# Three entries of a hand-written planner changed: ranks of the centring, the engine of one square, the load prices of one batch

## The chip, the cores and the metric

The kernel runs on one core of a Trainium2 chip. The core has TensorE (PE in the profile; PEld is its weight load), VectorE (DVE), ScalarE (ACT), GpSimd (POOL) and SyncE (SP, which here only issues DMAs). The metric is the device time of one execution in microseconds, as the median of five runs. One further execution is profiled.

## What is computed

Linear attention per batch and head, an RMS norm over each head, and on its result a feed-forward layer with the SoLU activation and a layer norm:

```
kv  = einsum('bhsd,bhse->bhde', k, v)            # 8 batches, 8 heads, 576 rows, 64 wide
out = einsum('bhsd,bhde->bhse', q, kv)
x   = out / sqrt(mean(out*out) + 1e-6) * g_norm  # per head; then 4608 tokens x 512
h   = x @ w_in                                   # 512 -> 1024
u   = h * softmax(h)
ln  = (u - mean(u)) / sqrt(var(u) + 1e-6) * g_ln
y   = ln @ w_out                                 # 1024 -> 512
```

## The kernel before

**Tiles and chunks.** The tokens go in nine chunks of 512: chunks 0 to 7 hold 512 rows of one batch each, and chunk 8 holds the last 64 rows of all batches. For a chunk `c`, `kv_mm` (L286) multiplies k and v into PSUM, `kv_copy` (L304, L306) casts the result to bf16, three copies for each half, `qT_mm` (L314) and `qT` (L321, L323) transpose q (chunks 4 to 8 use a transposing DMA from SP instead, L328), and `o_mm` (L348) multiplies. Then come a square on ScalarE (`sq`, L363), the mean by a matmul (`s_mm`, L369), `ln` and `ex` on ScalarE (L373, L377; chunk 0 uses one reciprocal root, L383) and `x` on VectorE (L390).

**The feed-forward part.** Each chunk has eight blocks `f` of 128 features. `h_mm(c, f)` (L471) is four matmuls, `exp(c, f)` (L479) runs on ScalarE, `u(c, f)` (L486) multiplies h by its exponential on VectorE, `usq(c, f)` (L495 on ScalarE, L497 on GpSimd) squares u, and `es(c, n)` (L503) adds two exponentials on GpSimd. When all of u, usq and es of a chunk are there, `sums(c)` (L537) adds them over the features by matmuls, `turn` and `stats` (L545 to L558, VectorE) and `rstd` (L562, L564, ScalarE) make one factor for each token. `out(c, m, half)` (L585) multiplies u by `w_out_sb` in two halves of four matmuls, `ob(c, m)` (L617) scales the result, and `store` (L626) sends it off from SP.

**Centring.** The mean over the features is taken out of the weights once: `w_mean` (L570) makes the mean of g_ln times w_out in a PSUM bank of the tag `out`, and eight `w_center(f)` (L576, VectorE) write `w_out_sb[:, f]`. `out(c, m, 0)` needs `w_center` 0 to 3, `out(c, m, 1)` needs 4 to 7, and the bank of the mean comes free with the last of them.

**Buffers.** PSUM has two banks for `h`, two for `out`, two for `o`, one for `s` and one for `misc`. `kv_mm(c)` for c > 1 takes `misc` and `s`. In SBUF there are three slots each for k, v and q, four for e, two each for u, usq, es and x.

**The order.** The order of the program on every engine is made by a small planner, `Plan.order` (L33 to L81). Each piece of work is added with its engine, a length, a rank, what it needs, and the buffers that it takes first or uses. The planner keeps a time at which each engine is free. It takes again and again the piece that could start first, and among those with the same start the one with the lower rank, and it writes that piece's instructions. These times are the planner's own; on the chip only the order remains, and each instruction waits for its real inputs.

**Loads in the planner.** A load on GpSimd's queue has a length (the issue) and a `load` (the transfer). All loads form one queue: a load ends at `queue = max(queue, t + length + 1.0) + load` (L72) and counts as landed some time later (L73). At most eight loads are under way (L55). Loads of k, v and q for batches 0 and 1 come in two halves, for the others whole. Two more things steer them: `behind` (L249) holds the loads of batch b until `h_mm(b - 3, ...)`, and from batch 5 on also until `gate(b - 1)` (L335), a tiny GpSimd copy that reads the last element of q of the batch before, so that GpSimd passes it only when that load has landed.

**Ranks and engines.** The rank of a piece is the chunk in which it is due, with the block in eighths: `h_mm(c, f)` has c + f/8, `u(c, f)` that plus 0.04, so `u(0, 6)` has 0.79 and `u(0, 7)` 0.915. The squares of chunk 0 have -0.6. `qT(1, hf)` (ACT) has -0.9 + 0.8 (0.12 + 0.1 hf), and `kv_mm(3)` 1.4.

The two expressions around which the change turns:

```
first=[] if g else [(name, b)], load=2.9 / n if b < 4 else 3.5)
...
engine = "act" if f in {0: (2, 4, 6, 7), 1: (), NC - 1: (1, 3, 5, 6, 7)}.get(c, (2, 6)) else "pool"
```

Of the kernel before, what the change touches and what calls it, by code (L numbers as in the profile page):

```python
# [18 lines left out]
class Plan:  # L19
# [13 lines left out]
    def order(self):  # L33
        free, done, queue, lanes, mode = {}, {}, 2.5, [], {}
        held = {tag: [] for tag in self.bufs}
        waiting = {n: set(p[4]) for n, p in self.pieces.items()}
        behind = {}
        for n, needs in waiting.items():
            for m in needs:
                behind.setdefault(m, []).append(n)  # L40
        ready = [n for n, needs in waiting.items() if not needs]
        order = []
        while ready:
            best = None
            for n in ready:
                engine, length, rank, fn, needs, first, load = self.pieces[n]
                t = max([free.get(engine, 0.0)] + [done[m] for m in needs])
                more = {}
                for key in first:
                    old = held[key[0]] + more.setdefault(key[0], [])  # L50
                    more[key[0]].append(key)
                    if len(old) >= self.bufs[key[0]]:
                        last = self.users[old[-self.bufs[key[0]]]]
                        t = max([t] + [done.get(m, 1e9) for m in last])
                if load and len(lanes) >= 8:  # L55
                    t = max(t, lanes[-8])
                if t < 1e8 and (best is None or (t, rank) < best[:2]):
                    best = (t, rank, n)
            t, rank, n = best
            engine, length, rank, fn, needs, first, load = self.pieces[n]  # L60
            ready.remove(n)
            for key in first:
                held[key[0]].append(key)
            if engine == "pe":

                tiling = n[0] if n[0] in ("kv_mm", "o_mm", "sums") else "full"
                length += 0.1 if mode.get(engine, tiling) != tiling else 0.0
                mode[engine] = tiling
            free[engine] = t + length
            done[n] = t + length + {"pe": 0.2, "sp": 2.5}.get(engine, 0.12) + (2.0 if n[0] == "qT" and engine == "sp" else 1.0 if n[0] == "gate" else 0.0)  # L70
            if load:
                queue = max(queue, t + length + 1.0) + load  # L72
                done[n] = queue + 1.3  # L73
                lanes.append(done[n])
            order.append(fn)
            for m in behind.get(n, ()):
                waiting[m].discard(n)
                if not waiting[m]:
                    ready.append(m)
        assert len(order) == len(self.pieces)  # L80
        return order  # L81
# [3 lines left out]
def kernel(  # L85
# [27 lines left out]
    NC = B + 1  # L113
# [19 lines left out]
    plan = Plan({**banks, **bufs})  # L133
# [105 lines left out]
    def heads(c):  # L239

        return (slice(0, 4), slice(4, 8)) if c < 2 else (slice(0, 8),)
# [5 lines left out]
    for b in range(B):  # L247
        at = b - 9.0 if b > 1 else (-2.0, -1.5)[b]
        behind = [] if b < 2 else [("h_mm", 0, 0)] if b == 2 else ([("gate", b - 1)] if b - 1 in XBAR else []) + [("h_mm", b - 3, 2 if b == 3 else 0)]  # L249
        for g, hs in enumerate(heads(b)):  # L250
            part = 0.1 * g
            n = len(heads(b))
            for i, (name, src) in enumerate((("k", k), ("v", v))):
                plan.add((name, b, g), "pool", 0.75 if n == 1 else 0.6, at + part + 0.01 * i,
                         lambda name=name, src=src, b=b, hs=hs: load_kv(name, src, b, hs),
                         behind, uses=[(name, b)] if g else [],
                         first=[] if g else [(name, b)], load=2.9 / n if b < 4 else 3.5)
            plan.add(("q", b, g), "pool", 0.9 if n == 1 else 0.7, at + part + (0.02 if b < 2 else 0.1),
                     lambda b=b, hs=hs: load_q(b, hs), behind,
                     uses=[("q", b)] if g else [], first=[] if g else [("q", b)], load=2.7 / n if b < 4 else 3.3)  # L260
        plan.add(("q_last", b), "pool", 0.6, 2.0 + 0.5 * b, lambda b=b: load_q_last(b),
                 [("h_mm", 2 + b // 2, 4 * (b % 2))], load=0.5)
    for half in range(2):
# [133 lines left out]
    for c in range(NC):  # L397
# [4 lines left out]
        if c < B:  # L402
            for xs in ((0,), (1,)) if c < 2 else ((0, 1),):
                g = xs[0]
                rg = r + 0.5 * w * g
                plan.add(("kv_mm", c, g), "pe", 0.65, rg, lambda c=c, xs=xs: kv_mm(c, xs), [("k", c, g), ("v", c, g)],
                         uses=[("k", c), ("v", c)], first=[(kv_tag(c, x), "kv", c, x) for x in xs])
                for x in xs:
                    for part in range(3):
                        plan.add(("kv", c, x, part), kv_engine(c, x), 0.25, rg + 0.05,  # L410
                                 lambda c=c, x=x, part=part: kv_copy(c, x, part), [("kv_mm", c, g)],
                                 uses=[(kv_tag(c, x), "kv", c, x)])
        if c in XBAR:
            plan.add(("qT", c), "sp", 1.8, r - 0.1, lambda c=c: q_turn(c),
                     [("q", c, 0)] if c < B else [("q_last", b) for b in range(B)],
                     uses=[("q", c)] if c < B else [], first=[("qT", c)])
# [3 lines left out]
        for hf in range(2):  # L420
            g = group(c, hf)
            tag = ("out", "h")[c] if c < 2 and hf else "o"
            if c not in XBAR:
# [7 lines left out]
                         first=[] if hf else [("qT", c)])  # L431
# [3 lines left out]
                     uses=[("qT", c)], first=[(tag, c, hf, z) for z in range(2)])  # L435
            for z in range(2):
                i = (c, hf, z)
                rz = r + w * (0.4 + 0.5 * hf + 0.12 * z)
                if (c, hf) in COPIED and z:
                    plan.add(("oc", i), "dve", 0.62, rz, lambda i=i: o_copy(*i), [("o_mm", c, hf)],  # L440
                             uses=[(tag, *i)], first=[("oc", i)])
                    plan.add(("sq", i), "pool", 1.05, rz + 0.01, lambda i=i: o_sq_copy(*i), [("oc", i)],
                             uses=[("oc", i)], first=[("osq", i)])
                else:
                    plan.add(("sq", i), "act", 0.57, rz, lambda i=i: o_sq(*i), [("o_mm", c, hf)],
                             uses=[(tag, *i)], first=[("osq", i)])
                stag = "h" if i in ((0, 0, 1), (0, 1, 0)) else "s"
                plan.add(("s_mm", i), "pe", 0.22, rz + 0.02, lambda i=i, stag=stag: s_mm(i, stag), [("sq", i)],
                         uses=[("osq", i)], first=[(stag, i)])
                if c == 0:  # L450
                    plan.add(("ex", i), "act", 0.6, rz + 0.04, lambda i=i: s_rsqrt(*i), [("s_mm", i)],
                             uses=[(stag, i)], first=[("rst", i)])
                else:
                    plan.add(("ln", i), "act", 0.6, rz + 0.03, lambda i=i: s_ln(*i), [("s_mm", i), "table"],
                             uses=[(stag, i)], first=[("lss", i)])
                    plan.add(("ex", i), "act", 0.6, rz + 0.04, lambda i=i: s_exp(*i), [("ln", i)],
                             uses=[("lss", i)], first=[("rst", i)])
                plan.add(("x", i), "dve", 0.67, rz + 0.06, lambda i=i: x_mul(*i),
                         [("ex", i)] + ([("x", (c, 0, 0))] if (hf, z) != (0, 0) else []),
                         uses=[(tag, *i), ("rst", i)] + ([("x", c)] if (hf, z) != (0, 0) else []),  # L460
                         first=[("x", c)] if (hf, z) == (0, 0) else [])
# [44 lines left out]
    for c in range(NC):  # L506
        for f in range(NF):
            r = c + f / 8
            plan.add(("h_mm", c, f), "pe", 0.87, r, lambda c=c, f=f: h_mm(c, f),
                     [("w_in", f // 4), *[("x", (c, *i)) for i in xs]], uses=[("x", c)], first=[(h_bank(c, f), "h", c, f)])  # L510
            plan.add(("exp", c, f), "act", 0.57, r + 0.02, lambda c=c, f=f: h_exp(c, f),
                     [("h_mm", c, f), "table"] + ([("exp", c, f - 1)] if f % 2 else []), uses=[(h_bank(c, f), "h", c, f)] + ([("e", c, f // 2)] if f % 2 else []),
                     first=[] if f % 2 else [("e", c, f // 2)])
            plan.add(("u", c, f), "dve", 0.62, r + 0.04, lambda c=c, f=f: h_u(c, f),
                     [("exp", c, f)] + ([("u", c, 0)] if f else []), uses=[(h_bank(c, f), "h", c, f), ("e", c, f // 2)] + ([("u", c)] if f else []),
                     first=[] if f else [("u", c)])
            engine = "act" if f in {0: (2, 4, 6, 7), 1: (), NC - 1: (1, 3, 5, 6, 7)}.get(c, (2, 6)) else "pool"
            plan.add(("usq", c, f), engine, 0.57 if engine == "act" else 1.05, r + 0.15 if c else -0.6,
                     lambda c=c, f=f, engine=engine: u_sq(c, f, engine), [("u", c, f)] + ([("usq", c, 0)] if f else []),
                     uses=[("u", c)] + ([("usq", c)] if f else []), first=[] if f else [("usq", c)])  # L520
            if f % 2:
                n = f // 2
                plan.add(("es", c, n), "pool", 1.28, r + 0.1, lambda c=c, n=n: e_sum(c, n),
                         [("exp", c, f)] + ([("es", c, 0)] if n else []), uses=[("e", c, n)] + ([("es", c)] if n else []),
                         first=[] if n else [("es", c)])
# [49 lines left out]
    def w_center(f):  # L575
        nc.vector.scalar_tensor_tensor(  # L576
            out=w_out_sb[:, f, :], in0=w_out_f[:, f, :].bitcast(FP32), scalar=g_ln_sb[:, f:f + 1],
            in1=T["mean"][:, :], op0=MUL, op1=SUB,
        )
# [39 lines left out]
    def store(c, m):  # L619
# [3 lines left out]
        else:  # L623
# [4 lines left out]
    plan.add("w_mean", "pe", 2.0, -0.5, lambda: [w_mean(f) for f in range(NF)], ["w_out", "g_mean", ("o_mm", 0, 1)],  # L628
             first=[("out", "mean")])
    for f in range(NF):  # L630
        plan.add(("w_center", f), "dve", 0.67, 0.05 + 0.12 * f, lambda f=f: w_center(f), ["w_mean"], uses=[("out", "mean")])
    for c in range(NC):
        r, rs = (c + 1, c + 1) if c else (0.55, -0.5)
        parts = [[("u", c, f) for f in range(NF)], [("usq", c, f) for f in range(NF)], [("es", c, n) for n in range(NF // 2)]]
# [1 line left out]
                 uses=[("u", c), ("usq", c), ("es", c)], first=[("misc" if c else "h", "sum", c)])  # L636
        plan.add(("turn", c), "dve", 0.25, rs + 0.14, lambda c=c: sums_turn(c), [("sums", c)],
                 uses=[("misc" if c else "h", "sum", c)])
        plan.add(("stats", c), "dve", 0.65, rs + 0.16, lambda c=c: stats(c), [("turn", c)], uses=[("misc" if c else "h", "sum", c)])
        plan.add(("rstd", c), "act", 0.45, rs + 0.17, lambda c=c: rstd(c), [("stats", c)])  # L640
        for x in range(2 if c == NC - 1 else 0):
            engine = ("dve", "act")[x]
# [3 lines left out]
                     uses=[("h", "acc", x)] + ([("ob", c, 3)] if x else []), first=[] if x else [("ob", c, 3)])  # L646
# [46 lines left out]
```

## Time and profile before

| What | Value |
|---|---|
| median of 5 runs | 196.78 us (195.87 to 197.02) |
| the profiled execution, its time | 196.78 us |
| the profiled execution, its span | 195.0 us |
| granted TensorE clock | 1.0 of full speed throughout |
| ScalarE busy, 40 to 50 us | 8.89 of 10 us |
| DMA share, 10 to 60 us | 1.23 to 1.30 in each 10 us |
| loads on GpSimd's queue | 17.30 MB in 20112 packets |
| stores, 34 of 256 KB from SP | 2.8 us to landing (median) |

The span is the time from the first to the last instruction of the profiled execution; what lies around it is start and end of the program. Busy times are those of one engine; several engines work at once, so they do not add up to the span. A wait is idle time of an engine in front of an instruction, put down to whatever came last for that instruction. The chain of work that ended last is followed back from the last instruction: at each step to what released it. [...] In the timelines L-numbers are lines of the kernel, and a group "x8" stands for eight instructions in a row.

### The profile page before, as it was taken

Reading aid. Unit: us, or ns where it says so; the run is one execution under the profiler, and the core shown is the slowest. Engines: PE = TensorE matmul, PEld = TensorE weight load, DVE = VectorE, ACT = ScalarE, POOL = GpSimd, SP = SyncE. Lnnn points to the kernel's source line nnn. Section 1 sums busy time; section 2 is a strip of 40 time slices with the busy share of each in tenths; the row PEclk is TensorE's granted clock in tenths of the full one; section 3 lists DMA queues with packets and bytes.
Section 4 is the critical chain, followed back from the end, with each engine's and each line's share of the span. In section 5 each row is a group of like instructions: output and inputs, shape, how many; then the busy total and the mean of one; then the engine's idle time right before and its main releaser. Section 6 shows DMA issues by size and latency. Waiting matters only on the chain.

```text
span 195.0 us, 5441 instructions
## 1 busy us (share of the span) xinstructions
PE 178.6 (92%) x2282; PEld 88.5 (45%) x2282; DVE 122.5 (63%) x241; ACT 140.2 (72%) x244; POOL 129.2 (66%) x140
## 2 busy tenths in 40 slices
PE   7698896889689988999999999999999999999990
PEld 2243364554354443454445445445445554544560
DVE  1255679296866858648675965867594757665450
ACT  2027887979978897978889796988779496556420
POOL 7963599700789996796796977577385838846200
PEclk9999999999999999999999999999999999999999
DMA  3999999999995999999999955156111111211216
GB/s 51 178 201 275 348 204 204 203 207 269 229 204 86 166 202 198 173 206 201 206 186 199 235 105 137 59 113 173 54 54 57 57 54 57 108 57 54 109 23 196
DMA packets 36040, 29.71 MB, mean 152 GB/s; under 512 B 11816, under 2 KB 30512, under 8 KB 36016
## 3 DMA queue, kind: packets, MB, share of 16 engines
q0 software_dynamic: 20112, 17.30, 55.2%
q1 hardware_dynamic: 15616, 11.67, 20.7%
q10 hardware_dynamic: 288, 0.39, 0.6%
q8 instruction: 18, 0.29, 0.6%
q14 instruction: 6, 0.05, 0.1%
HBM read 32.51 MB, written 9.44 MB: 215 GB/s over the span
## 4 chain that ended last, share of the span: by engine, by line
PE 69%; DMA 15%; POOL 7%; ACT 3%; issue 2%; DVE 1%; POOLq 0%
PE out_ps L585 27%; PE h_ps L471 26%; DMA q_sb<-in_q_dram 11%; PE misc_ps L537 4%; DMA v_sb<-in_v_dram 4%; PE s_ps L369 3%; PE o_ps L348 3%; POOL usq_sb L497 2%; POOL k_sb L212 2%; PE misc_ps L286 1%; POOL es_sb L503 1%; PE misc_ps L193 1%; PE h_ps L595 1%; PE o_ps L585 1%; POOL v_sb L212 1%
## 5 line engine op out<-in xcount | busy, mean ns | idle before, releaser
L471 PE MATMUL h_ps<-x_sb,w_in_sb 128*128 128x512 bf16 x276 | 70.1, 379 | 1.1 <-DVE x_sb L390 1.1
L585 PE MATMUL out_ps<-w_out_sb,u_sb 128*128 128x512 bf16 x272 | 68.8, 379 | 2.0 <-DVE ob_sb L617 1.6
L497 POOL TENSOR_TENSOR usq_sb<-u_sb 128x512 bf16<-128x512 bf16 x51 | 52.9, 1045 | 22.0 <-DVE u_sb L486 21.8
L503 POOL TENSOR_TENSOR es_sb<-e_sb 128x512 bf16<-128x512 f32 x36 | 45.8, 1272 | 26.2 <-ACT e_sb L479 26.1
L486 DVE TENSOR_TENSOR u_sb<-h_ps,e_sb 128x512 bf16<-128x512 f32 x69 | 47.3, 687 | 25.1 <-ACT e_sb L479 24.6
L479 ACT ACTIVATE e_sb<-h_ps,zero_t 128x512 f32<-128x512 f32 x69 | 47.1, 683 | 13.7 <-PE h_ps L471 13.3
L471 PEld LDWEIGHTS <-w_in_sb 128*128 128x128 bf16 x288 | 27.2, 98 | 34.6 <-issue 4.0
L585 PEld LDWEIGHTS <-u_sb 128*128 128x128 bf16 x280 | 26.4, 98 | 33.5 <-issue 3.6
L390 DVE SCALAR_TENSOR_TENSOR x_sb<-o_ps,g_rep,rst_sb 128x512 bf16<-128x512 f32 x32 | 23.9, 750 | 11.0 <-ACT rst_sb L377 10.9
L617 DVE TENSOR_SCALAR ob_sb<-out_ps,rstd 128x512 f32<-128x512 f32 x33 | 24.5, 746 | 8.5 <-PE out_ps L585 4.4
L363 ACT ACTIVATE osq_sb<-o_ps,zero_t 128x512 bf16<-128x512 f32 x31 | 19.7, 682 | 13.8 <-PE o_ps L348 13.8
L373 ACT ACTIVATE lss_sb<-s_ps,eps_t 128x512 f32<-128x512 f32 x32 | 22.0, 688 | 2.6 <-PE s_ps L369 2.6
L377 ACT ACTIVATE rst_sb<-lss_sb,zero_t 128x512 f32<-128x512 f32 x32 | 23.2, 726 | 0.7
L495 ACT ACTIVATE usq_sb<-u_sb,zero_t 128x512 bf16<-128x512 bf16 x21 | 15.2, 722 | 6.1 <-DVE u_sb L486 6.0
L369 PE MATMUL s_ps<-osq_sb,head_mean 128*128 128x512 bf16 x34 | 12.9, 380 | 0.8 <-ACT lss_sb L373 0.4
L537 PEld LDWEIGHTS <-stat_sel 128*32 128x32 bf16 x720 | 10.1, 97 | 3.7 <-issue 3.2
L286 PE MATMUL misc_ps<-v_sb,k_sb 64*64 64x64 bf16 x360 | 7.6, 194 | 3.5 <-DMA v_sb<-in_v_dram 3.5
L193 PE MATMUL s_ps<-zeros 128*128 128x512 bf16 x28 | 9.1, 448 | 1.4 <-DVE zero_t L158 1.2
L220 POOL DMA_DIRECT2D q_sb<-in_q_dram x10 | 8.6, 856 | 2.3 <-DMA w_in_sb<-in_moe_w_in_dram 1.5
L212 POOL DMA_DIRECT2D k_sb<-in_k_dram x10 | 7.9, 787 | 3.4 <-DMA w_in_sb<-in_moe_w_in_dram 1.9
L286 PEld LDWEIGHTS <-k_sb 64*64 64x64 bf16 x576 | 6.8, 107 | 7.1 <-issue 7.1
L304 DVE CAST kvd<-misc_ps 64x128 bf16<-64x128 f32 (+1 forms) x24 | 6.9, 287 | 3.0 <-PE misc_ps L286 2.7
(86 smaller groups left out, 133.1 us busy)
## 6 DMA issues: line engine op xcount, KB each, us to landing
out_dram<-ob_sb SPq DMA_DIRECT2D x34, 256.0 KB, 2.8
k_sb<-in_k_dram POOLq DMA_DIRECT2D x6, 576.0 KB, 11.4
v_sb<-in_v_dram POOLq DMA_DIRECT2D x6, 576.0 KB, 11.9
q_sb<-in_q_dram POOLq DMA_DIRECT2D x6, 512.0 KB, 14.1
w_out_f<-in_moe_w_out_dram POOLq DMA_DIRECT2D x1, 2048.0 KB, 16.5
k_sb<-in_k_dram POOLq DMA_DIRECT2D x4, 288.0 KB, 11.9
v_sb<-in_v_dram POOLq DMA_DIRECT2D x4, 288.0 KB, 12.2
q_sb<-in_q_dram POOLq DMA_DIRECT2D x4, 256.0 KB, 12.1
```

The lines of the kernel that those rows point to most:

```text
L363: nc.scalar.activation(out=t[:, :], in_=T[("o", *i)].rearrange("p a b c -> p (a b c)"), func=AF.Square, bias=zero_t[:, :])
L369: nc.tensor.matmul(t[:, :], head_mean[:, :], T["osq", i][:, :], start=True, stop=True)
L373: nc.scalar.activation(out=t[:, :], in_=T["s", i][:, :], func=AF.Ln, bias=eps_t[:, :])
L377: nc.scalar.activation(out=t.rearrange("p a b c -> p (a b c)"), in_=T["lss", i][:, :], func=AF.Exp, scale=-0.5, bias=zero_t[:, :])
L390: nc.vector.scalar_tensor_tensor(out=T["x", c][:, 2 * hf:2 * hf + 2, z], in0=T["o", c, hf, z][:, :, :, :], scalar=g_rep[:, :], in1=T["rst" ...
L471: nc.tensor.matmul(t[:, :], w_in_sb[:, dt, f * 128:(f + 1) * 128], T["x", c][:, dt].rearrange("p a b c -> p (a b c)"), start=(dt == 0), st ...
L479: nc.scalar.activation(out=T["e", c, f // 2][:, f % 2, :], in_=T["h", c, f][:, :], func=AF.Exp, bias=zero_t[:, :])
L486: nc.vector.tensor_tensor(out=T["u", c][:, f, :], in0=T["h", c, f][:, :], in1=T["e", c, f // 2][:, f % 2, :], op=MUL)
L497: nc.gpsimd.tensor_tensor(out=dst, in0=src, in1=src, op=MUL)
L503: nc.gpsimd.tensor_tensor(out=T["es", c][:, n, :], in0=e[:, 0, :], in1=e[:, 1, :], op=ADD)
L585: nc.tensor.matmul(T["acc", c, m][:, :], T["u", c][:, f, m * 128:(m + 1) * 128], w_out_sb[:, f, :], start=(f == 0), stop=(f == NF - 1),)
L617: nc.vector.tensor_scalar_mul(out=t[:, :], in0=T["acc", c, m][:, :], scalar1=T["rstd", c][:, m:m + 1])
```

## The change

There are three edits, all in what the planner is told. No instruction is added, and one changes its engine.

- The ranks of `w_center(f)` go from 0.05 + 0.12 f to 0.8 + 0.04 f. Against `u(0, 7)` (0.915) the first three are lower and the other five higher.
- The squares of chunk 0 on ScalarE go from blocks 2, 4, 6, 7 to blocks 1, 3, 5, 6, 7. GpSimd keeps 0, 2, 4 instead of 0, 1, 3, 5.
- The loads of batch 3 are priced as those of the later batches (3.5 and 3.3 instead of 2.9 and 2.7), and count as landed 5.3 instead of 1.3 after their turn in the queue. The condition is on the second part of a piece's name, so `("q_last", 3)` gets the 5.3 too.

```
             if load:
                 queue = max(queue, t + length + 1.0) + load
-                done[n] = queue + 1.3
+
+                done[n] = queue + (5.3 if n[1] == 3 else 1.3)
                 lanes.append(done[n])
...
-                         first=[] if g else [(name, b)], load=2.9 / n if b < 4 else 3.5)
+                         first=[] if g else [(name, b)], load=2.9 / n if b < 3 else 3.5)
...
-                     uses=[("q", b)] if g else [], first=[] if g else [("q", b)], load=2.7 / n if b < 4 else 3.3)
+                     uses=[("q", b)] if g else [], first=[] if g else [("q", b)], load=2.7 / n if b < 3 else 3.3)
...
-            engine = "act" if f in {0: (2, 4, 6, 7), 1: (), NC - 1: (1, 3, 5, 6, 7)}.get(c, (2, 6)) else "pool"
+            engine = "act" if f in {0: (1, 3, 5, 6, 7), 1: (), NC - 1: (1, 3, 5, 6, 7)}.get(c, (2, 6)) else "pool"
...
-        plan.add(("w_center", f), "dve", 0.67, 0.05 + 0.12 * f, lambda f=f: w_center(f), ["w_mean"], uses=[("out", "mean")])
+        plan.add(("w_center", f), "dve", 0.67, 0.8 + 0.04 * f, lambda f=f: w_center(f), ["w_mean"], uses=[("out", "mean")])
```

## The prediction

> **What bounds the kernel now.** I read first the busy shares and one wide stretch of the windows, then the waits of TensorE, then the chain that ended last, then the timelines of single engines from 20 to 75 us.
>
> ```profile
> span 195.0 us, 5441 instructions
> ...
> PE 178.6 (92%) x2282; PEld 88.5 (45%) x2282; DVE 122.5 (63%) x241; ACT 140.2 (72%) x244; POOL 129.2 (66%) x140
> ```
>
> The windows by stage (columns: stretch, its length, busy time of PE, PEld, DVE, ACT, POOL, granted clock, DMA share, GB/s):
>
> ```profile
> 28.00:34.00 6.00, 4.46 (x99) 2.94 (x98) 5.95 (x10) 4.55 (x10) 5.96 (x7) 1.00 1.27 204
> 46.00:56.00 10.00, 7.27 (x115) 3.49 (x113) 6.95 (x12) 8.29 (x16) 5.99 (x6) 1.00 1.24 237
> 68.00:75.00 7.00, 5.61 (x99) 2.79 (x98) 4.82 (x14) 6.88 (x15) 6.58 (x7) 1.00 1.30 200
> 75.00:185.00 110.00, 110.00 (x1357) 52.93 (x1358) 72.80 (x137) 84.40 (x147) 75.78 (x75) 1.00 0.55 123
> ```
>
> From 75 to 185 us PE is busy 110.00 of 110.00. All of TensorE's idle time after the warm-up lies before 75 us, and the change alters no matmul. So the end moves by what PE gains or loses before 75 us. Its waits between 29 and 75 us (waiter, what it waited for, total, times, longest):
>
> ```profile
> PE misc_ps L286 <- DMA v_sb<-in_v_dram: 2.0, 2, 1.1
> PE out_ps L585 <- DVE ob_sb L617: 1.6, 2, 1.0
> PE misc_ps L314 <- DMA q_sb<-in_q_dram: 1.3, 1, 1.3
> PE misc_ps L314 <- ACT kvd L306: 0.9, 1, 0.9
> PE out_ps L585 <- DVE w_out_sb L576: 0.4, 1, 0.4
> PE s_ps L369 <- ACT lss_sb L373: 0.4, 1, 0.4
> PE s_ps L369 <- ACT osq_sb L363: 0.3, 1, 0.3
> PE o_ps L348 <- ACT qT_sb L321: 0.2, 1, 0.2
> ```
>
> Together 7.1 us. Two are the loads of chunk 3: PE stands at kv_mm(3) until 49.95 (1.06) and at qT_mm(3,0) until 54.21 (1.32). The chain shows the second, and a chain over ScalarE to the 0.96 us wait at 74:
>
> ```profile
> 32.11 22.05 DMA q_sb<-in_q_dram
> ...
> 54.21 0.62 PE misc_ps L314 x8
> ...
> 69.90 0.72 ACT usq_sb L495
> ...
> 73.23 0.75 DVE ob_sb L617
> ```
>
> **How I get the new order.** Each engine runs in program order, and the planner sets it: the piece that can start first by its costs, the lower rank at a tie. I walk this rule with the changed ranks and costs from chunk 0 on, and take all times of the profile's clock from the trace. Around h_mm(1,0) the planner's clock is 0.9 us behind the profile's (45.86 against 46.78).
>
> **Step 1, centring.** No instruction is added. The eight centrings take 0.667 us each:
>
> ```profile
> 28.01 5.34 DVE L576 SCALAR_TENSOR_TENSOR w_out_sb<-w_out_f,g_ln_sb,out_ps 128x512 bf16<-128x512 f32 x8
> 33.27 0.68 DVE L486 TENSOR_TENSOR u_sb<-h_ps,e_sb 128x512 bf16<-128x512 f32 x1
> ```
>
> Rank 0.915 of u(0,7) now lies between w_center(2) (0.88) and w_center(3) (0.92). DVE: three centrings to 30.01, u(0,7) 30.01 to 30.69 (its exp ends at 29.45), five centrings to 33.95, which is where u(0,7) ends today. out(0,0,0) starts at 30.75 and reaches its fourth matmul at 31.40; w_center(3) ends at 31.3, so the later centring is just hidden (if the cover is gone, 0.1 to 0.7). Gain: u(0,7) is 3.3 us earlier, and with it its square and sums(0).
>
> **Step 2, squares.** ScalarE takes five of chunk 0, GpSimd three. POOL loses one of 1045 ns: es(0,3), now ending at 35.5, ends near 34.6; k/v/q(3) and the loads behind keep their order, k(3) 0.3 later and k(4) 1.0 earlier, into a backlog. ACT gains one of 722 ns (0.62 from start to start). Its usq(0,1) pushes exp(0,3) from 23.43 to about 23.87; that is hidden, since exp(0,7) waits for h_mm(0,7) behind the eight mean matmuls of PE, and stays at 28.76. The price is usq(0,7): it needs u(0,7) (30.69) and stands ahead of the copy qT(1,0) in ACT's queue. The copy goes from 30.95 to 31.36 and o_mm(1,0) from 32.01 to 32.42: 0.41 lost. Behind the square on ACT wait only that copy and the two squares of o; PE waits for both.
>
> It is paid back: ACT has no usq(0,7) at 33.99 any more, and PE runs s_mm(1,0,0), out(0,0,1) and sums(0) at about 34.6 instead of 36.96. PE then waits 0.55 for ACT's third kv(1,1) copy (36.4). kv_mm(2) still starts at 39.17, since v(2) lands at 39.06 (issue 25.56 plus 13.5). But o_mm(1,1) is then behind PE, rstd(0) ends at 39.35, ob(0,0) at 40.1 instead of 40.7, and out(0,2,0) starts at 40.15 instead of 40.76. ACT's order (two squares, then three kv copies) keeps s_mm(1,1,0) at 42.05 against 42.49, and h_mm(1,0) at 46.3 against 46.78. **Steps 1 and 2: 0.45.** Bounds: minus 0.6 (the 0.41 and no payback, plus the 0.16 idle time before ACT's ln at 44.50) and plus 0.9 (the waits of 0.6 and 0.3 before 46.6 both gone). I take 0.45, nearest to the shifts that I followed.
>
> **Step 3, the loads of chunk 3.** The planner has them land at 43.8, 46.7 and 49.4; with 3.5, 3.5, 3.3 and 5.3 it is 48.4, 51.9 and 55.2. In the trace, issue plus time to landing is 44.5 (29.32 + 15.2), 49.8 (30.13 + 19.7) and 54.2 (32.11 + 22.1). The DMA share is over 1.2 throughout, so issuing earlier or later by 0.3 hardly moves these. kv_mm(3) moves from behind s_mm(2,0,1) to behind h_mm(1,5), near 54.1; qT_mm(3,0) to behind s_mm(2,1,1), near 56.8. Both loads have landed 4.3 and 2.6 us before. What is late next: h_mm(1,2) needs u(1,0), at about 49.35, so PE idles 0.95 where it idled 1.06; but it now computes h there, and h_mm(1,4), held until 54.67, starts near 51.9. After that ACT sets the pace: ln, exp, ex, three kv(3,1) copies (0.81), exp(1,5) at 56.1, exp(1,7) at 59.2. h_mm(2,0) comes near 59.85 instead of 61.21. **Steps 1 to 3: 1.36**, 0.9 of it from step 3. Bounds of step 3: 0 (ACT, busy 8.29 of 10 us, takes all) and 2.4 (both waits).
>
> [...]
>
> **Step 4, what follows at 62 to 74.** q(4) is now planned at 61.5 instead of 60.28 (the trace has 37.11 + 24.2 = 61.3). So gate(4) and the issues of chunk 5 fall behind usq(1,7) and usq(2,0) on POOL. usq(1,7) ends at 62.8 of the planner's clock instead of 66.0, sums(1) starts at 63.6 instead of 66.6, rstd(1) is done near 67 instead of 70.3, and out(1,2,0) finds its bank free. The 0.96 before 74.03 and the 0.41 before s_mm(3,1,1) at 71.83 can both go: bounds 0 and 1.37. I take 1.15, since the walk shows PE without a gap there. The price: three loads of chunk 5 are issued 2.2 us later (62.83 today). v(5) lands at 73.4, kv_mm(5) starts at 88.2; that covers it. If the cover were gone, gate(5) (76.50, q(5) landed at 76.2) would hold POOL's squares by up to 2.
>
> **Sum.** 195.0 - 0.45 - 0.9 - 1.15 = 192.5 of span. The profiled execution took 196.78 with a span of 195.0, so 1.78 lie around it; it is also the median of the five runs. Forecast: 194.3 us.
>
> **Rivals.**
> - *ScalarE takes the room.* For it: 8.29 of 10 us busy from 46 to 56. Step 3 gives 0.2, step 4 0.4, steps 1 and 2 0.3: 195.9. Against it: h_mm(1,4) waits for a load today, not for ACT.
> - *Slower: the square at usq(0,7).* It holds qT(1,0), and the 0.62 of ACT is never paid back, while the three kv(3,1) copies (0.81) now stand ahead of exp(1,5) and hold h_mm(1,7). 0.41 + 0.81 = 1.2 slower: 198.0. It decides if h_mm(1,0) starts after 47.2 and nothing is gained at 74. Against it: es(0,3) and u(0,7) both come earlier, so sums(0) must too.
> - *It does not do what it says.* v(3) or q(3) is waited for still, because chunk 0's stores start 0.6 earlier and delay them by over 2.6 us. Step 3 gives 0, the others 1.0: 195.8. Against it: four stores of 256 KB are issued before 47.4 in both kernels.
>
> [...]
>
> **Chances.** Forecast 0.66 (193.2 to 195.3), ScalarE 0.17 (195.3 to 196.6, about half within 0.3%), slower 0.12 (196.9 to 198.5), load still late 0.05 (195.3 to 196.2). 0.3% (0.6 us) is about what a measurement of this kernel can tell from no change. Faster: 0.66 + 0.08 + 0.05 = 0.79; same 0.09; slower 0.12. The range 193.0 to 196.6 holds the forecast's bounds and both cases of a small gain; it leaves out the slower case and what exceeds the bounds.
>
> **What would show it.** Right: no wait of PE for v_sb or q_sb after 45 us; u(0,7) near 30.0; sums(0) near 34.6; o_mm(1,0) 0.4 later; h_mm(2,0) near 59.9; no wait for ob_sb at 70 to 74; PE without a gap to 185. Wrong: PE gaps at 48 to 58 of 3 us again, now behind ACT; o_mm(1,1) after 39.75; POOL idle at a gate; a new gap after 75.

## The result and the profile after

| | before | changed |
|---|---|---|
| median | 196.2 us, 94 runs (195.23 to 197.88) | 196.91 us, 52 runs (193.37 to 201.14) |
| ratio of the changed kernel to before | | 0.9963, 95% interval [0.9949, 0.9978] |
| the profiled execution: time, span, mean clock | 196.78 us, 195.0 us, 1.000 | 199.55 us, 197.8 us, 0.990 |

The forecast was 194.3 us, 1.2% faster. What came is 0.4% faster by the ratio, 0.4% slower by the median of all runs, and a kernel whose time differs by 4% from run to run. The ratio leaves out runs more than 1.5% above a kernel's fastest, and with them 32 of the changed kernel's 52, so that the median of all runs tells more about this kernel than the ratio; why such runs are long is traced below in one of them.

The page of the changed kernel, span and busy shares:

```profile
span 197.8 us, 5443 instructions
...
PE 181.7 (92%) x2282; PEld 89.1 (45%) x2282; DVE 122.4 (62%) x241; ACT 140.7 (71%) x245; POOL 128.6 (65%) x139
```

The windows of the changed kernel, the same stretches and columns as before (stretch, length, busy time of PE, PEld, DVE, ACT, POOL, clock, DMA share, GB/s). The DMA share is the profile's mean busy share of the core's 16 DMA engines; here it is 1.22 to 1.30 in each 10 us from 10 to 60 us, so 1 is not its upper end.

```profile
28.00:34.00 6.00, 4.42 (x101) 2.89 (x101) 5.22 (x9) 5.01 (x10) 5.98 (x7) 1.00 1.27 204
46.00:56.00 10.00, 8.91 (x115) 3.99 (x114) 6.78 (x12) 9.21 (x18) 7.31 (x7) 1.00 1.25 220
68.00:75.00 7.00, 6.80 (x32) 2.98 (x31) 5.73 (x11) 6.89 (x13) 6.99 (x8) 1.00 1.14 200
75.00:185.00 110.00, 105.70 (x1296) 50.56 (x1295) 70.23 (x133) 82.91 (x145) 73.31 (x73) 0.98 0.56 121
```

From 46 to 56 us PE idles 1.09 us where it idled 2.73, from 68 to 75 us 0.20 where it idled 1.39. Over 28 to 75 us the idle time falls from 7.17 to 3.95. That idle time would go there is what was forecast. The last row is what was not: PE was busy for all 110.00 us from 75 to 185, and now idles 4.30 of them, at a mean clock of 0.98.

The waits of PE in the changed kernel, first from 29 to 75 us, then from 75 to 190 (waiter, what it waited for, total, times, longest):

```profile
PE h_ps L472 <- DVE u_sb L487: 1.3, 3, 0.9
PE misc_ps L315 <- ACT kvd L307: 0.9, 1, 0.9
PE s_ps L370 <- ACT osq_sb L364: 0.6, 2, 0.3
PE misc_ps L287 <- DMA v_sb<-in_v_dram: 0.5, 1, 0.5
PE o_ps L349 <- ACT qT_sb L322: 0.5, 1, 0.5
```

```profile
PE misc_ps L538 <- POOL usq_sb L498: 4.3, 1, 4.3
```

The waits for chunk 3's loads and the two for `ob_sb` are gone. (The one wait for `v_sb` is that of chunk 2, at 38.9.) One wait has come: `sums(3)` needs a square of GpSimd. GpSimd's timeline in the changed kernel (start, length, operation, idle time before it and what ended it) shows why the square is late:

```profile
64.47 0.83 POOL L213 DMA_DIRECT2D k_sb<-in_k_dram  x1
...
66.02 0.90 POOL L221 DMA_DIRECT2D q_sb<-in_q_dram  x1
...
82.31 0.18 POOL L336 COPY landed<-q_sb 1x1 bf16<-1x1 bf16 x1 [4.15 <-DMA q_sb<-in_q_dram]
...
85.90 0.91 POOL L221 DMA_DIRECT2D q_sb<-in_q_dram  x1
...
100.54 0.18 POOL L336 COPY landed<-q_sb 1x1 bf16<-1x1 bf16 x1 [4.20 <-DMA q_sb<-in_q_dram]
100.68 1.03 POOL L498 TENSOR_TENSOR usq_sb<-u_sb 128x512 bf16<-128x512 bf16 x1
```

The same places before, with no idle time ahead of the gates:

```profile
64.37 0.90 POOL L220 DMA_DIRECT2D q_sb<-in_q_dram  x1
...
76.50 0.18 POOL L335 COPY landed<-q_sb 1x1 bf16<-1x1 bf16 x1
...
94.56 0.18 POOL L335 COPY landed<-q_sb 1x1 bf16<-1x1 bf16 x1
94.69 1.03 POOL L497 TENSOR_TENSOR usq_sb<-u_sb 128x512 bf16<-128x512 bf16 x1
```

The tiny copies are the gates. gate(5) stands 4.15 us on GpSimd until q(5) is there, 16.2 us after its issue (11.8 before). These are the landings of that load, first before, then changed:

```profile
DMA to landing us min/median/max: 11.8/11.8/11.8
DMA to landing us min/median/max: 16.2/16.2/16.2
```

The loads of chunk 6, issued behind it, are late in turn (q(6) 14.5 us after its issue, 11.9 before). gate(6) stands 4.20 us, and behind it in GpSimd's order is `usq(3, 7)`, the last square that `sums(3)` needs: PE has come as far as this square at 97.47, and it starts at 100.68. Before, `sums(3)` was begun only at 102.67, 8 us behind gate(6).

The wait costs more than its length. Windows of the changed kernel around it (columns as above):

```profile
97.40:101.70 4.30, 0.07 (x7) 0.00 (x0) 0.56 (x1) 1.05 (x2) 1.16 (x3) 0.98 0.41 55
101.70:104.00 2.30, 2.24 (x24) 1.03 (x24) 1.37 (x6) 0.45 (x2) 2.30 (x5) 0.50 1.09 213
104.00:105.00 1.00, 1.00 (x4) 0.36 (x3) 0.74 (x2) 0.14 (x1) 1.00 (x2) 0.54 0.70 52
```

After 4.3 us without matmuls the granted clock is 0.50 until about 105. In the next run a wait of 1.85 us left the clock at 1.00. In another run below, that of the kernel whose gate reads an earlier q, waits of 2.35 and 3.04 us were each followed by 3.4 us at 0.50 (the second from 118.4, 1.5 us behind its wait). These are its windows there:

```profile
94.50:97.90 3.40, 3.40 (x15) 1.21 (x15) 0.75 (x1) 1.88 (x3) 3.40 (x5) 0.50 1.14 277
118.40:121.80 3.40, 3.40 (x10) 1.19 (x9) 1.39 (x2) 2.10 (x4) 0.33 (x1) 0.50 1.24 270
```

Waits of 2.65 us (chunk 1's stores behind the transposing DMA, 103.28) and 2.96 us (ranks and square alone, 50.79) left it at 1.00. So the length of the wait alone doesn't decide, and what else does isn't shown.

Starts of the sums on PE put all of it into one account (us; the last three rows are experiments told below):

| kernel | sums(1) | sums(3) | sums(4) | sums(8) |
|---|---|---|---|---|
| before | 68.93 | 102.67 | 118.22 | 184.50 |
| changed | 62.77 | 96.44 | 120.12 | 187.38 |
| changed, run again | 62.53 | 96.22 | 115.97 | 183.23 |
| before, gates behind squares | 65.49 | 97.67 | 115.40 | 182.65 |
| changed, gates behind squares | 63.41 | 97.09 | 114.81 | 182.07 |

The changed kernel needs 23.68 us from sums(3) to sums(4), and 17.72 with the gates out of the way: 5.96 more, of which 4.29 is the wait. The other 1.67 is put down to the half clock; 3.15 us of work at 0.50 (101.76 to about 104.9) cost about 1.6, by estimate from the two clocks; four matmuls of `out` took 1.89 us there (102.42) and 1.03 at 1.00 (105.37). The changed kernel was 0.65 ahead at sums(3), because near the start of the program the first v landed at 7.39 us in that execution, and PE did not wait for it; in the other it landed at 8.65 and PE waited 1.39 (8.51 and 1.50 in the profile of before). This differs between executions whose order is the same that far, and is no part of the change. So the end, by sums(8): 2.43 gained by the changed order with the gates out of the way, 0.65 gained at the start, 5.96 lost, together 2.88 later (184.50 to 187.38).

### The profile page after: what moved, and what is told of

It reads as the page before. It is cut to its first block, busy times and chain, and to the rows that moved or that the text cites. A ratio compares the mean times of both kernels' runs of the same rounds, so it can differ in the third digit from the quotient of the medians.

```text
span 197.8 us, 5443 instructions
## 1 busy us (share of the span) xinstructions
PE 181.7 (92%) x2282; PEld 89.1 (45%) x2282; DVE 122.4 (62%) x241; ACT 140.7 (71%) x245; POOL 128.6 (65%) x139
## 4 chain that ended last, share of the span: by engine, by line
PE 53%; DMA 32%; POOL 6%; ACT 3%; issue 2%; DVE 2%; POOLq 0%
DMA q_sb<-in_q_dram 28%; PE out_ps L586 20%; PE h_ps L472 19%; DMA v_sb<-in_v_dram 4%; PE misc_ps L538 3%; PE o_ps L349 2%; PE s_ps L370 2%; POOL k_sb L213 2%; POOL usq_sb L498 2%; POOL v_sb L213 1%; DVE w_out_sb L577 1%; PE misc_ps L194 1%; PE out_ps L571 1%; PE h_ps L596 1%; PE o_ps L586 1%
## 5 line engine op out<-in xcount | busy, mean ns | idle before, releaser
L586 PE MATMUL out_ps<-w_out_sb,u_sb 128*128 128x512 bf16 x272 | 69.8, 383 | 0.0
L498 POOL TENSOR_TENSOR usq_sb<-u_sb 128x512 bf16<-128x512 bf16 x50 | 51.9, 1042 | 23.0 <-DVE u_sb L487 22.9
L364 ACT ACTIVATE osq_sb<-o_ps,zero_t 128x512 bf16<-128x512 f32 x31 | 20.3, 684 | 14.7 <-PE o_ps L349 14.7
L496 ACT ACTIVATE usq_sb<-u_sb,zero_t 128x512 bf16<-128x512 bf16 x22 | 15.8, 719 | 6.2 <-DVE u_sb L487 6.2
L194 PE MATMUL s_ps<-zeros 128*128 128x512 bf16 x28 | 9.9, 479 | 1.4 <-DVE zero_t L159 1.2
L563 ACT ACTIVATE lv<-vare,zero_t 128x4 f32<-128x4 f32 x9 | 2.7, 295 | 10.3 <-DVE vare L559 10.2
L538 PE MATMUL misc_ps<-usq_sb,stat_sel 128*32 128x128 bf16 x256 | 5.2, 220 | 4.3 <-POOL usq_sb L498 4.3
```

Of the source, the lines that this page charges most:

```text
L364: nc.scalar.activation(out=t[:, :], in_=T[("o", *i)].rearrange("p a b c -> p (a b c)"), func=AF.Square, bias=zero_t[:, :])
L498: nc.gpsimd.tensor_tensor(out=dst, in0=src, in1=src, op=MUL)
L538: nc.tensor.matmul(T["sum", c][32 * j:32 * j + 32, 0, :], stat_sel[:, i, :], cols, start=(part == 0 and n == 0), stop=(part == 2 and n == ...
L586: nc.tensor.matmul(T["acc", c, m][:, :], T["u", c][:, f, m * 128:(m + 1) * 128], w_out_sb[:, f, :], start=(f == 0), stop=(f == NF - 1),)
```

## The experiments

The theory to test: sums(1) and its `rstd` come some 6 us earlier, so chunk 1's stores (4 times 256 KB) start at 68.0 instead of 74.0, beside chunk 5's loads, which start 1.6 later. SP's timeline shows the stores, first before, then changed:

```profile
74.00 3.92 SPq L626 DMA_DIRECT2D out_dram<-ob_sb  x3
...
68.02 8.45 SPq L627 DMA_DIRECT2D out_dram<-ob_sb  x4
```

(The fourth store of before follows at 80.49.) By the theory, these stores delay chunk 5's loads, q(5) lands late, the gates hold GpSimd, and a square behind gate(6) holds PE. Rivals: the loads are late for another reason; the gates don't matter and the lateness itself is the loss; some part of the change loses time by itself.

**The changed kernel once more**, without an edit:

> The changed kernel once more, nothing altered. Theory (gate): GpSimd stands at gate(5) until q(5) lands and at gate(6) until q(6) lands; usq(3,7) is the next piece behind gate(6), so sums(3) holds TensorE, 4.3 us in the profile after; the length follows the landing of q(6), so the stall differs from run to run, 1 to 5 us, and the time with it, 193.5 to 200. Rival (clock): TensorE's granted clock drops first and by itself, and the stall at sums(3) has the same length in every profile.

196.77 us, 10 runs (195.48 to 199.74), ratio 1.0024 [0.9991, 1.0057]. The profiled execution has a span of 193.7: the gates stand 1.59 and 3.84 us, and PE's timeline shows the shorter wait; the clock behind it is 1.00 (99.1 to 103 us):

```profile
99.09 0.24 PE L538 MATMUL misc_ps<-usq_sb,stat_sel 128*32 128x128 bf16 x4 [1.85 <-POOL usq_sb L498]
```

sums(3) to sums(4) takes 19.75 here, 2.03 more than without the wait. So one and the same kernel loses about 2 or about 6 us in these two executions. The difference begins at q(5): it landed 13.6 us after its issue here and 16.2 there, so gate(5) stood 1.59 us instead of 4.15, and chunk 6's loads were issued 2.8 us earlier (81.56 against 84.34). q(6) itself took 14.6 and 14.5 us, about the same. What makes q(5) later in one run than in another isn't settled. The rival, a clock that drops first and by itself, doesn't fit: the wait differs in length, and in the longer one the clock was 0.98 during the wait and 0.50 only behind it.

**The gate reads the q of the chunk before**, so that it never waits:

```
-        nc.gpsimd.tensor_copy(landed[:, :], T["q", c][0:1, H - 1, 3, D - 1:D])
+        nc.gpsimd.tensor_copy(landed[:, :], T["q", c - 1][0:1, H - 1, 3, D - 1:D])
```

> The changed kernel, with the same order on every engine; only gate(c) reads q of batch c-1, which landed long before, so that GpSimd passes it without waiting. Theory (gate): GpSimd's idle time of 4.15 and 4.20 us before the gates is gone, so is the 4.3 us wait at sums(3) and the drop of the granted clock behind it; the time is about 196.2 - 3.2 = 193.0 us, 192.3 to 194.0. Rival (GpSimd has too much to do): the squares still end late, PE waits 3 us or more at sums(3), the time stays at 195 to 199. Rival (the loads themselves are late): the wait moves to kv_mm(6) or o_mm(5,0), the time stays above 194.5.

199.67 us, 6 runs (193.33 to 202.87; too uneven for an interval). No wait at a gate and none at the sums, but PE now waits for the transposed q, by its waits from 76 to 185 us:

```profile
PE o_ps L349 <- DMA qT_sb<-q_sb: 5.4, 2, 3.0
```

The transposing DMA of q(5) goes out at 80.04 and chunk 6's loads right behind it, from 80.22 (80.30 against 78.03 before); chunk 7's loads go out from 95.81, while q(6) is still under way until 103.65. q(6) lands 21.9 us after its issue. The transposing DMAs take 4.06 and 5.88 us on SP's queue (2.37 and 2.82 before) and land 14.4 and 13.2 us after their issue (4.4 and 4.7 before). So the lateness finds another victim when the gate is merely opened: holding the loads back has a use. The rival (the wait moves to `o_mm`) held here.

**No stores of chunk 1** (512 rows of the output are left out):

```
+        if c == 1:
+            return
```

> The changed kernel without the four stores of chunk 1 (those rows of the output are left out); the order is otherwise the same. Theory (collision): the stores of chunk 1, now issued from 70 us on instead of 74, share the DMA engines with the loads of chunk 5 and make q(5) land 16.2 us after its issue instead of 11.8; without them it lands in 11 to 12 us, gate(5) waits less than 1 us, gate(6) too, and sums(3) holds PE for less than 1 us: 192.5 to 194.0. Rival (the loads are late because they are issued 1.7 us later): q(5) still takes 14 us or more, gate(5) waits 3 to 4 us, and the time stays at 195 to 199.

194.53 us, 4 runs, ratio 0.9908 [0.9889, 0.9926]. The loads are issued as late as in the changed kernel (q(5) at 65.80), but q(5) lands 11.2 us later instead of 13.6 or 16.2, and gate(5) waits for nothing:

```profile
DMA to landing us min/median/max: 11.2/11.2/11.2
...
77.89 0.18 POOL L336 COPY landed<-q_sb 1x1 bf16<-1x1 bf16 x1
```

gate(6) waits 0.23, and no sums wait. So the stores are what makes chunk 5's loads late. In the changed kernel these stores are late as well: the four land 6.7 us after their issue (median), where the median of all stores of 256 KB from SP is 2.9. In what way they delay the loads, by sharing the DMA engines, as was expected here, or otherwise, isn't shown.

**The parts of the change alone.** Centring and square without the new prices:

```
-                done[n] = queue + (5.3 if n[1] == 3 else 1.3)
-                         ... load=2.9 / n if b < 3 else 3.5)
-                     ... load=2.7 / n if b < 3 else 3.3)
+                done[n] = queue + 1.3
+                         ... load=2.9 / n if b < 4 else 3.5)
+                     ... load=2.7 / n if b < 4 else 3.3)
```

> The kernel before with the new ranks of the centring and the new engine of the square, without the load prices. By the prediction's steps 1 and 2: 0.45 faster than before, PE waiting for v(3) and q(3) about 1.1 and 1.8 us. By the gate theory: chunk 5's loads keep their place ahead of usq(1,7), so no gate holds PE, and the time is 195.2 to 196.0. Rival (the square ahead of qT(1,0) costs 0.4 and is not paid back): 196.4 to 196.8.

196.42 us, 12 runs, ratio 1.0019 [0.9994, 1.0044]: nothing. The time is that of the rival and not of the theory, but the rival's reason isn't seen, since sums(0) starts at 34.02 instead of 36.96. PE runs ahead and gives it back: it waits 2.96 us for v(3) at 50.79 and 1.42 for `ob_sb` at 73.49. No gate waits.

The changed kernel with the old prices, but the later landing (5.3) kept:

```
-                         ... load=2.9 / n if b < 3 else 3.5)
-                     ... load=2.7 / n if b < 3 else 3.3)
+                         ... load=2.9 / n if b < 4 else 3.5)
+                     ... load=2.7 / n if b < 4 else 3.3)
```

> The changed kernel, but the loads of batch 3 keep 2.9 and 2.7; only the later landing (5.3) stays. kv(3) and qT(3,0) then have the place of the changed kernel, while q(4) is planned 1.75 us earlier and gate(4) and the issue of chunk 5's loads come 1.7 us earlier. Theory (collision of chunk 5's loads with chunk 1's stores): PE gains the same 3 us before 75 us, q(5) is issued near 64.3 instead of 66.0 and lands earlier by as much, gate(6) has more of GpSimd's work ahead of it and no square of chunk 3 is held long: stall at sums(3) under 1.5 us, 193.3 to 195.0. Rival (only stores matter, the issue does not): the time stays as with the change, 195 to 199.

199.07 us, 6 runs, ratio 1.0121 [1.0083, 1.0158]. The gates wait 2.23, 2.21 and 4.29 us, and sums(1), sums(2) and sums(3) 0.29, 1.26 and 2.11: the expectation missed, since the planner now put `usq(2, 7)` straight behind gate(5) as well. It fits the mechanism, but was not foreseen. Nor did chunk 5's loads go out earlier (q(5) at 65.80 against 66.02), since gate(4) now waited for q(4); so this run says nothing about the time of issue.

The new prices without the centring and the square:

```
-            engine = "act" if f in {0: (1, 3, 5, 6, 7), ...
+            engine = "act" if f in {0: (2, 4, 6, 7), ...
-        plan.add(("w_center", f), "dve", 0.67, 0.8 + 0.04 * f, ...
+        plan.add(("w_center", f), "dve", 0.67, 0.05 + 0.12 * f, ...
```

> The kernel before with the new load prices of batch 3 alone (ranks and squares as before). The prediction had 0.9 for the loads and 1.15 for what follows. Theory (collision): PE's waits for v(3) and q(3) go, but rstd(1) and so the stores of chunk 1 come 2 to 3 us earlier, chunk 5's loads 2 us later; q(5) lands late, gate(5) stands directly ahead of usq(2,7), so that already sums(2) holds PE, and sums(3) again: 196 to 199. Rival (the extra square of the change is what loads GpSimd's queue wrongly): no stall, 194.5 to 195.5.

198.71 us, 10 runs (196.1 to 201.45), ratio 1.0085 [1.0054, 1.0115]. The profile is that of the shortest run: gate(5) waits 0.16, gate(6) 2.63, and the waits for v(3) and q(3) are gone. No sums wait there, where both `sums(2)` and `sums(3)` were expected to. The time came as expected, then, but why the other runs are longer isn't shown.

**The gate counts as passed at once in the planner**, which issues chunk 5's loads 2 us earlier:

```
-            ... + (2.0 if n[0] == "qT" and engine == "sp" else 1.0 if n[0] == "gate" else 0.0)
+            ... + (2.0 if n[0] == "qT" and engine == "sp" else 0.0)
```

> The changed kernel, but the planner takes a gate as done when it ends, not 1.0 us later, so that the loads of chunk 5 stand directly behind gate(4) and not behind usq(2,0) as well; the gates still wait for q. Theory: chunk 5's loads are issued 1.1 us earlier, gate(5) and gate(6) wait 1 to 2 us less, sums(3) holds PE up to 2 us less: 194 to 196. Rival (stores alone set the landing of q(5)): no gain, 195 to 199.

196.2 us, 12 runs, ratio 0.9999 [0.9983, 1.0015]. The loads start as early as before the change (k(5) at 62.48), and q(5) still lands 15.7 us after its issue; the gates wait 2.58 and 2.77, `sums(2)` 1.44. So the 1.6 us of later issue are not needed for a late q(5); the stores are.

**Chunk 1's stores behind the transposing DMA of q(5)**:

```
-                     [("ob", c, m)], uses=[("ob", c, m)])
+                     [("ob", c, m)] + ([("qT", 5)] if c == 1 else []), uses=[("ob", c, m)])
```

> The changed kernel with the stores of chunk 1 placed behind the transposing DMA of chunk 5 in the store queue, so that they start after q(5) has landed; nothing is left out. Theory (collision): q(5) lands 11 to 12 us after its issue, no gate holds a square of chunk 3, no stall of PE over 1 us; but the four result buffers of chunk 1 are held until 82, where chunk 2's first results need them. 193.0 to 194.5 if these come in time. Rival (the DMA work is only moved and hits chunk 6's loads): q(6) lands late, gate(6) and sums(3) stall as before, 195 to 199.

199.93 us, 6 runs, ratio 1.0174 [1.013, 1.0219]. q(5) lands 10.6 us after its issue and gate(5) waits for nothing, which shows the stores' part a second time with nothing left out. But seven stores go out from 78.6 to 91.1, beside chunk 6's loads, gate(6) stands 6.18 us, and sums(3) waits 2.65:

```profile
97.82 0.18 POOL L336 COPY landed<-q_sb 1x1 bf16<-1x1 bf16 x1 [6.18 <-DMA q_sb<-in_q_dram]
```

The rival held: the collision was only moved.

**The gate behind the squares.** If late loads cost time only because a square stands behind the gate, one more need in the planner should be enough. It leaves the gate in force:

```
-                 plan.add(("gate", c), "pool", 0.15, r - 12.0, lambda c=c: load_gate(c), [("q", c, 0)], uses=[("q", c)])
+                 plan.add(("gate", c), "pool", 0.15, r - 12.0, lambda c=c: load_gate(c), [("q", c, 0), ("usq", c - 3, 7)], uses=[("q", c)])
```

> The changed kernel with one more need: gate(c) also waits in the planner for usq(c-3,7), so that GpSimd meets gate(6) only behind the last square of chunk 3. My theory (late loads of chunk 5 and 6 cost time only because squares stand behind a gate on GpSimd): q(5) and q(6) still land 13 to 16 us after their issue and the gates may still wait, but sums(3) no longer waits for a square; span about 195.0 - 3.2 = 191.8 to 192.5, time 193.3 to 194.2, and little spread. Rival (the late loads find the next victim): loads of chunk 7 are issued later and PE waits at kv_mm(7), qT or o_mm(6, 0), or squares of chunk 4 wait behind the gate instead: 195.5 or more.

194.32 us, 6 runs (194.03 to 194.38), ratio 0.9889 [0.9854, 0.9924]. The span is 192.5; the time is 0.1 above the expected range. gate(5) still waits 1.35 and gate(6) 4.16, as GpSimd's timeline of this kernel shows, but the last square of chunk 3 is now ahead of it:

```profile
94.86 1.04 POOL L498 TENSOR_TENSOR usq_sb<-u_sb 128x512 bf16<-128x512 bf16 x1
...
100.56 0.18 POOL L336 COPY landed<-q_sb 1x1 bf16<-1x1 bf16 x1 [4.16 <-DMA q_sb<-in_q_dram]
```

PE has no wait after 75 us, apart from gaps of 0.16 in front of groups of three matmuls where four are issued, taken here for missing records. The six runs lie within 0.35 us. The last link of the theory is shown: loads as late (q(5) 14.3 us after its issue, q(6) 15.2), no loss.

The same edit on the kernel before:

> The same need of the gates added to the kernel before. My theory: there the gates did not wait (q(5) lands 11.8 us after issue), so it changes nothing: 196.2 within 0.3%. Rival (the place of the gate is worth something by itself, by letting squares pass the issues of loads): 194.5 to 195.5, and then part of what the run before this one shows would not be a repair of the change.

194.83 us, 7 runs (194.43 to 195.42), ratio 0.992 [0.9889, 0.9951]. The theory said no effect, and the rival held. The waits of PE from 28 to 76 us tell where it comes from:

```profile
PE misc_ps L286 <- DMA v_sb<-in_v_dram: 2.6, 2, 1.3
...
PE out_ps L585 <- DVE ob_sb L617: 0.3, 1, 0.3
```

The loads of chunk 3 are waited for as before. But gate(4) and chunk 5's loads are behind `usq(1, 7)`, sums(1) starts at 65.49 instead of 68.93, and the 0.96 us wait for `ob_sb` at 74 and the 0.41 at 71.8 are gone. That is the prediction's step 4, without steps 1 to 3. Here, too, q(5) is late now (13.5 us after its issue) and gate(6) stands 2.33 us, and no wait of PE follows.

Both planner edits of the gate on the changed kernel (behind the squares, and passed at once):

> As the first of these three, and the gate counts as passed at once in the planner (the +1.0 taken out), which put the loads of chunk 5 ahead by some 2 us before. My theory: q(5) lands near 79 as before, gates wait, no square behind them: the time of the first of the three within 0.4 us. Rival: loads issued back to back share the engines and land later, 195 or more.

194.11 us, 6 runs (193.82 to 194.32), ratio 0.988 [0.9848, 0.9911], within 0.4 us of the one without: as expected. Its median is the lowest of all.

Last, centring and square with the gates behind the squares, and the old prices:

> The kernel before with the changed ranks of the centring, the changed square of chunk 0 and the gates behind the squares; the loads of chunk 3 stay priced as before. It splits the 0.5 us between the two runs with this gate, 194.83 (neither ranks nor prices) and 194.32 (both). My theory (what steps 1 and 2 gain is lost again at v(3), which lands near 50.4 whatever is done): near 194.8, with a wait of 2 to 3 us at kv_mm(3), and the new prices are worth the 0.5. Rival (steps 1 and 2 carry the 0.45 that the prediction gave them): 194.4 or less, and the new prices add nothing once the gate is there.

195.1 us, 12 runs (194.6 to 196.96), ratio 0.9969 [0.9943, 0.9995]. Centring and square add nothing to the gate (0.992 without them); the new prices do (0.9889 with all). The time came as expected, the place only in part: the profiled execution, one of the short ones, waits 0.55 us at kv_mm(3) and 1.14 at qT_mm(3, 0), where 2 to 3 were expected.

## Why the prediction was wrong

The forecast was a gain of 2.5 us. The median rose by 0.7, and even by the ratio only 0.4% of the 1.2% came. The step that failed is the price in step 4: late loads of chunk 5 were put at nothing ("that covers it"). They came late, by chunk 1's earlier stores and not by their own later issue, and through gate(5), gate(6) and the square behind it they cost 5.96 us in the profiled execution and 2.03 in the repeat. With the gates behind the squares the changed kernel takes just the time that was forecast (forecast 194.3, span 192.5; measured 194.32 and 192.5). In part that is luck: three quarters of that gain come from the gates' new place, which the change doesn't have, and the median of before is 196.2 and not the 196.78 from which the forecast was counted. The steps, against the two profiles:

- **Step 1, centring: right.** DVE's timeline of the changed kernel has three centrings, `u(0, 7)`, five centrings, as walked. With the gates behind the squares, where the start of the program is nearly that of before, `u(0, 7)` is at 30.03; 30.01 was forecast. The changed kernel itself:

```profile
29.24 0.69 DVE L487 TENSOR_TENSOR u_sb<-h_ps,e_sb 128x512 bf16<-128x512 f32 x1
29.84 3.38 DVE L577 SCALAR_TENSOR_TENSOR w_out_sb<-w_out_f,g_ln_sb,out_ps 128x512 bf16<-128x512 f32 x5
```

- **Step 2, squares: right in its places, nothing by itself.** (By block, five squares change their engine and not one: 1, 3 and 5 go to ScalarE, 2 and 4 to GpSimd. In number ScalarE gains one, as the prediction's sum has it.) PE's wait for the qT copy goes from 0.24 to 0.47 (0.23 lost, 0.41 forecast), and, with the gates behind the squares, sums(0) starts at 34.8 (34.6 forecast) and h_mm(1, 0) at 46.22 (46.3). But the 0.45 reach the end only if something else lets them: alone they are waited away at v(3), and with the gates repaired they add nothing either.
- **Step 3, the loads of chunk 3: right.** No wait for v(3) or q(3); PE waits 0.90 for `u(1, 0)` ahead of 48.66, where 0.95 was forecast. h_mm(2, 0) starts at 60.72 instead of the 59.85 forecast, but with four half blocks of `out(1, ...)` ahead of it where the kernel before has two.
- **Steps 1 to 3 together were forecast at 1.36: too much.** With the gates repaired on both sides they are worth 0.5 us (194.83 to 194.32).
- **Step 4, the gain: right in kind, 1.15 forecast.** The wait for `ob_sb` is gone. By the gate edit alone on the kernel before, where the same waits go, it is 1.5 us of the median and 1.85 at sums(8).
- **Step 4, the price: this is what failed.** The prediction said that three loads of chunk 5 are issued 2.2 us later, "v(5) lands 73.4, kv_mm(5) starts 88.2; that covers it". It took the landing of before (v(5) at 73.44 there) and set the 2.2 against the 14.8 us of room to kv_mm(5). It did not carry its own gain on: sums(1) earlier by 3 us in its own walk means stores of chunk 1 earlier, beside those loads. q(5) took 16.2 us. And it looked for the victim at kv_mm(5), where there was room, not in GpSimd's order, where gate(5) and gate(6) stand in front of squares. Its sentence on the lost cover had "up to 2" for gate(5); measured were 4.15 and 4.20 at two gates, 4.29 of PE, and 1.67 more behind it, at the half clock.
- **The sum.** 2.5 forecast; 2.43 by sums(8) with the gates repaired. The idle time of PE from 28 to 75 us fell by 3.2 in the changed kernel and by 3.0 with the gates repaired (to 4.16); where the other 0.6 stays isn't settled.
- **The rivals.** ScalarE didn't take the room (PE's idle time from 46 to 56 us fell by 1.6), the square at `usq(0, 7)` cost 0.23 and was paid back, and the change did what it says. The loss came by a mechanism that none of them named, but the list of signs had both of its marks: POOL idle at a gate, and a new gap after 75.

That the stores delay the loads (no stores of chunk 1, stores moved) and that the gates pass the delay to PE through the squares behind them (gates behind squares) are shown. Not settled: why the landing of q(5) differs between runs of one kernel, which waits of 2 to 3 us are followed by a clock of 0.50, and what lengthens most runs with the prices alone.

## What to carry to other kernels

A stage that is made earlier also sends its stores earlier (here from 68.0 us on instead of 74.0): before a gain is booked, follow what it releases onto the DMA queues and see which loads it meets there. An instruction that waits for a DMA holds what stands behind it in its engine's order (here gate(6) stood 4.20 us ahead of `usq(3, 7)`), so list what stands there and put it after the work that somebody is about to wait for. And when a later wait could stop TensorE for some microseconds, price the clock that comes after it too (here some 3 us at 0.50 behind a wait of 4.29), and undo the suspected link on both kernels: here three quarters of the gain (1.5 of 2.05 us) lay in the gate's place and not in the change.

## What the runs showed of the hardware

- 1 MB of stores beside three loads of 576, 576 and 512 KB delayed the last of these from 10.6 or 11.2 us after its issue (stores moved, or left out) to 13.3 to 16.2 us, with the loads issued at 62.5 to 68 us.
- The time for which a DMA of half a megabyte is under way differed by 2.6 us between two executions of one kernel (q(5) 16.2 and 13.6). With two gates and a square behind it this became 3.9 us from sums(3) to sums(4) (23.68 and 19.75). That kernel's times spread over 4%; those of the kernel before, whose gates did not wait in its profile, over 1.4%.
- A wait of PE of 4.29 us was followed by some 3 us at a clock of 0.50, and waits of 2.35 and 3.04 us by 3.4 us each; waits of 1.85, 2.65 and 2.96 us were followed by none.
- A transposing DMA stood 1.9 to 3.1 us in SP's timeline (before and changed, 60 to 104 us) and landed 4.4 to 6.3 us after its issue. With loads of 576, 576 and 512 KB issued from 0.2 us behind it, it stood 4.06 us and landed after 14.4; with such loads issued 6 to 8 us ahead of it, 5.88 and 13.2.
